# Pre-LN attention and gated MLP on one core: a head in pairs, a plan that counts copies, tails that overtake

## The chip, the cores and the metric

The kernel runs on one core of a Trainium2 chip. The metric is the device time of one execution in microseconds. Engines are named as in the profile: PE is TensorE's matrix products, PEld its weight loads, DVE is VectorE, ACT is ScalarE, POOL is GpSimd, and SP is the engine whose queue issues the transfers.

## The reference

One transformer block over 2048 rows of width 640, in bfloat16, with 32 heads of 20:

```python
h = x + mha(layernorm(x), wqkv, wo)      # softmax(q k^T / sqrt(20)) v, 32 heads
g = layernorm(h) @ w_gate                # 640 x 1728
u = layernorm(h) @ w_up                  # 640 x 1728
out = h + (g * u) @ w_down               # 1728 x 640
```

## The kernel before, in words

**Attention.** Queries are cut into four blocks of 512 rows (0 to 3), heads into eight groups of four. A segment is one group of heads for one block of queries, or for half a block (256 rows). `SPLIT_1`, `SPLIT_2` and `SPLIT_3` say how many of the eight groups of blocks 1, 2 and 3 run whole; the other groups run first for the first half of the block (segments C, E, A) and then for the second half (D, F, B). Before the change block 3 ran two groups whole and six in halves.

Scores are made in units of 128 keys by 512 queries (`emit_S`, L723), three or two units at a time. ScalarE takes the exponential of most of them (`E`, L731). Every fourth to sixth unit goes to VectorE instead, which builds the exponential from bits (L743, L626 to L631). The products with the values (`emit_AV`, L870) accumulate in one bank `acc` and are copied out when a segment closes (L900). A sum row is inverted either by a chain of transfers through memory and POOL (`norm`) or, for a few urgent segments, on TensorE (`job_norm`, L792, L807, L823).

**Order of the work.** The whole instruction order is written out by a planner in Python when the kernel is built. It keeps clocks of its own for TensorE and VectorE (`clk["pe"]`, `clk["dve"]`) and the end of each exponential (`act_end`). After each step of scores it admits other TensorE work up to `limit_of(i)`. That other work lies in a queue `jobs`: transposes of the normed rows (`job_T`), projections of q, k and v (`job_proj`, `job_dense`, `job_V`), and the tails. `HURRY` adds 100 ns to the limit in block 3. Where no job can run, `idle_products` issues products whose results are not used (L1409, and L285 with `ident`). TensorE takes its queue strictly in the order written, so a job that waits also holds the scores behind it.

**Tails.** When every group of a block or half block is normed, `add_tail` appends a tail: loads of x and of the first weights (`load_tail` L1119, `load_w` L1175), the output product with the residual (`job_out`, L1132) and the second layer norm, the gated products (`job_glu`, L1202, results L1234) and the down product (`job_y`, L285 with `hh`, added at L1272, stored at L1279). Tails run one after the other in that queue.

**Head.** The first four row tiles are normed in two pairs. Each is transposed (L322), and then the first q and k products of group 0 run for both pairs (L972). They land in `pQ` and `pK` and are copied out in one piece of 512 columns each (L261 on ScalarE, L263 on VectorE). `WARM` products on the identity (L937) come before all of this; `pad` (L212) spreads the weights.

**End.** After the last exponential a loop flushes the value products and gives leftover jobs a turn (`work`). `last_tail` then does the tail of the last 256 rows: output products (L1332, L1334, L1338), the layer norm, transposes, glu (L1202 into `f`) and y. Between the norm's statistics and its application (L242) `fill()` runs all jobs left over.

Of the kernel before, what the change touches and what calls it, by code (L numbers as in the profile page):

```python
# [10 lines left out]
BF16 = mybir.dt.bfloat16  # L11
# [27 lines left out]
FP = 7  # L39
# [10 lines left out]
SPLIT_3 = 2  # L50
# [6 lines left out]
WARM = 40  # L57
# [15 lines left out]
EASE, HURRY = 0, 100  # L73
# [13 lines left out]
def kernel(  # L87
# [122 lines left out]
    def pad(c):  # L210
        fn = nc.gpsimd.tensor_copy if c > 2 else nc.scalar.copy
        fn(wpad[c][:, :, :, 0:DH], wqk_half(c, 0)[:, :, 0:GP * HPG * DH].rearrange("p m (h e) -> p m h e", e=DH))  # L212
# [117 lines left out]
    def job_lnT(t):  # L330
        yield from job_T(lns[t], lnT[:, :, t * P:(t + 1) * P])

# [6 lines left out]
    def job_proj(m, g, ch):  # L339
        yield ROUND * KT  # L340
        ps = bank()
        for c in range(KT):
            by_cols(ps[:], wslice(m, g, c), lnT[:, c, ch * QB:(ch + 1) * QB], start=(c == 0), stop=(c == KT - 1))
            mm(ROUND)
            if c == KT - 1:
                evac_b("dve", kT[g][:, ch * QB:(ch + 1) * QB] if m else q_of(g, ch, 0, QB), ps[:], m)
                ev(QB, held["slot"])
            else:
# [4 lines left out]
    def job_dense(m, t, ch):  # L353
        yield ROUND * KT
        ps = bank()
        for c in range(KT):
# [47 lines left out]
    def job_V(t, half):  # L404
        yield 136 * KT
        ps = bank()
        for c in range(KT):
# [8 lines left out]


# [162 lines left out]
    def can_work(limit):  # L580
# [5 lines left out]
        start = max(clk["pe"], next_free()) + (SWITCH if clk["kind"] != "cols" else 0)  # L586
# [24 lines left out]
    def acc_rounds(i):  # L611
# [8 lines left out]
        return int(max(when(u) for _, u in got) <= clk["pe"] + SLACK)  # L620
# [208 lines left out]
    def when(u):  # L829
        return u[0] if u[4][0] == "d" else act_end[u[0]] + WAKE  # L830
# [15 lines left out]
    def emit_AV(i, rounds, flush=False, need=None):  # L846
        while rounds > 0 and acc["next"] < len(segs):
# [12 lines left out]
            clk["pe"] = max([clk["pe"]] + [when(u) for _, u in got])  # L860
            mm(ROUND * w // QB)
            rounds -= w / QB
            for q, u in got:
# [3 lines left out]
                ensure(("v", kt, g // (NG // 2)))  # L867
# [83 lines left out]

    for k in range(2):
# [7 lines left out]
    pad(2)  # L960
    first_T(1, "dve", lambda: bn(pair_mv[1], 1, xs[0][:, 3, :]))
    for c in (3, 4):
        pad(c)
    m32, r = rstd_act(pair_mv[1], 2)
    for k in range(2):
        apply1(2 + k, m32, r, k)
    first_T(2, "act")
    first_T(3, "dve")
    for pr in range(2):
        for m in (1, 0):  # L970
            for c in range(KT):
                nc.tensor.matmul(  # L972
                    (pQ, pK)[m][:, pr * HW:(pr + 1) * HW], lhsT=wslice(m, 0, c),
                    rhs=lnT[:, c, pr * HW:(pr + 1) * HW], start=(c == 0), stop=(c == KT - 1))
    warm = small.tile([P, 1], BF16, name="warm", tag="den")
    nc.scalar.activation(warm[:], ones[:], ACT.Exp)
    load_x(2)
    evac_b("act", kT[0][:, 0:QB], pK[:, 0:QB], 1)
    evac_b("dve", q_of(0, 0, 0, QB), pQ[:, 0:QB], 0)
# [110 lines left out]
    def open_late():  # L1090
# [8 lines left out]
        nc.vector.tensor_copy(late["if"][:], ident[:])  # L1099
# [449 lines left out]
```

## Time and profile before

| | us |
|---|---|
| median of 3 runs | 881.75 (880.72 to 882.86) |
| profiled execution, its time | 881.99 |
| its span, first to last instruction | 880.1 |
| PE busy | 827.3 (94%) |
| ACT busy | 799.7 (91%) |
| DVE busy | 702.9 (80%) |
| POOL busy | 190.4 (22%) |

Read it so: the span is the execution as the trace has it, and the 1.9 us between it and the execution's time lie outside of the instructions. Shares are means over stages that differ: a head without exponentials, a long loop in which ScalarE is nearly always busy, and an end in which TensorE works alone. In rows of the timeline the first number is the start, the second the duration, both in us; a bracket gives the idle time before the instruction and what ended it. In rows of stretches (start:end) the columns are the length and then busy time with instruction counts of PE, PEld, DVE, ACT and POOL, the granted TensorE clock, the DMA share and GB/s. In rows of groups the busy time and the mean ns of one instruction follow the bar. Rows of the chain have start, duration and what it was.

### The profile page before, as it was taken

The page shows a single profiled execution, that of the slowest core. Times are in us where ns is not written, and L with a number is a line of the kernel's source. Part 1 is how long each engine was busy: PE and PEld are TensorE (multiplying, and loading weights), DVE is VectorE, ACT ScalarE, POOL GpSimd, SP SyncE. Part 2 cuts the span into 40 slices and gives each one's busy share as a digit, 9 for nine tenths or more (in the row PEclk, how much of TensorE's full clock was granted, in tenths as well). Part 3 has the DMA queues.
Part 4 walks back from the last instruction along what each step waited for, and adds up shares of the span by engine and source line. Part 5 has one row for each costly group of instructions (what it writes and reads, how often), then busy time and mean ns, then how long its engine had stood idle before and what let it go on. Part 6 is the DMA issues. An engine that isn't in the chain of part 4 may idle for free.

```text
span 880.1 us, 34361 instructions
## 1 busy us (share of the span) xinstructions
PE 827.3 (94%) x15265; PEld 404.8 (46%) x15265; DVE 702.9 (80%) x1384; ACT 799.7 (91%) x710; POOL 190.4 (22%) x258
## 2 busy tenths in 40 slices
PE   7889999998999999999999999999999999999995
PEld 4333334332334334445444555555454556555774
DVE  6665779898778989888888889888888888988642
ACT  5889999999999999999999999999899999999530
POOL 2220001334413311222141214121301141113000
PEclk8989999999999999999999999999899999999999
DMA  6111230144212322201305131413510310031310
GB/s 184 33 58 46 67 94 13 34 108 124 63 56 64 115 75 61 52 10 39 97 25 140 26 98 30 116 38 105 126 35 15 106 39 23 18 92 49 81 45 19
DMA packets 93959, 57.62 MB, mean 65 GB/s; under 512 B 24236, under 2 KB 91692, under 8 KB 93804
## 3 DMA queue, kind: packets, MB, share of 16 engines
q1 hardware_dynamic: 93804, 55.36, 23.4%
q8 instruction: 121, 1.98, 0.9%
q14 instruction: 34, 0.28, 0.1%
HBM read 46.94 MB, written 8.16 MB: 63 GB/s over the span
## 4 chain that ended last, share of the span: by engine, by line
PE 48%; ACT 24%; DVE 21%; issue 5%; DMA 1%; SPq 0%; DVEq 0%; ACTq 0%
ACT E L731 24%; PE sc L723 12%; PE acc L870 10%; PE mi L1202 9%; PE mi L285 8%; DVE di L743 6%; PE mi L359 3%; DVE di L631 3%; DVE dm L626 2%; DVE st L218 2%; PE f L285 2%; PE f L1202 2%; DVE dt L628 2%; PE mi L723 1%; PE acc L1409 1%
## 5 line engine op out<-in xcount | busy, mean ns | idle before, releaser
L731 ACT ACTIVATE E<-sc 128x1536 bf16<-128x1536 f32 (+1 forms) x679 | 782.6, 1265 | 27.1 <-PE sc L723 13.4
L743 DVE TENSOR_SCALAR di<-mi 128x512 int16<-128x512 f32 x350 | 238.1, 685 | 65.9 <-PE mi L723 62.8
L870 PE MATMUL acc<-E,vx 128*32 128x256 bf16 (+1 forms) x2532 | 221.3, 315 | 2.7 <-DVE vx L256 2.1
L723 PE MATMUL sc<-qa,kT 21*128 21x256 bf16 (+1 forms) x1800 | 205.2, 320 | 13.9 <-ACT E L731 8.9
L723 PEld LDWEIGHTS <-kT 21*128 21x128 bf16 x3072 | 85.1, 91 | 219.1 <-issue 207.9
L768 POOL TENSOR_TENSOR rr<-rr,powers 128x8 f32<-128x8 f32 (+1 forms) x44 | 95.2, 2165 | 415.6 <-DMA rr<-sums 415.4
L870 PEld LDWEIGHTS <-vx 128*32 128x32 bf16 x3612 | 81.4, 95 | 106.3 <-issue 95.3
L631 DVE TENSOR_TENSOR di<-di,dm 128x1024 bf16<-128x1024 bf16 x175 | 122.9, 702 | 4.6
L723 PE MATMUL mi<-qa,kT 21*128 21x256 bf16 (+1 forms) x376 | 98.0, 311 | 2.5 <-DVE di L743 1.1
L626 DVE TENSOR_SCALAR dm<-di 128x1024 int16<-128x1024 int16 x175 | 78.9, 451 | 3.7
L870 PE MATMUL acc<-di,vx 128*32 128x256 bf16 (+1 forms) x540 | 77.8, 309 | 1.0 <-DVE di L631 0.9
L870 PE MATMUL acc<-dt,vx 128*32 128x256 bf16 (+1 forms) x540 | 78.1, 311 | 0.5 <-DVE dt L628 0.4
L628 DVE TENSOR_SCALAR dt<-di 128x1024 int16<-128x1024 int16 x175 | 75.9, 434 | 0.0
L723 PE MATMUL sc<-qb,kT 21*128 21x256 bf16 (+1 forms) x732 | 67.4, 290 | 2.8 <-ACT E L731 2.4
L285 PE MATMUL mi<-wd,hh 128*32 128x320 bf16 x1344 | 62.2, 300 | 1.0 <-DVE di L743 0.6
L1202 PE MATMUL mi<-ln2T,wg 128*32 128x256 bf16 (+1 forms) x1170 | 55.6, 298 | 1.9 <-DVE di L743 1.0
L1202 PE MATMUL mi<-ln2T,wu 128*32 128x256 bf16 (+1 forms) x1170 | 55.6, 303 | 0.9 <-DVE di L743 0.5
L285 PEld LDWEIGHTS <-hh 128*32 128x32 bf16 (+1 forms) x1456 | 45.6, 96 | 18.0 <-issue 8.1
L1202 PEld LDWEIGHTS <-wu 128*32 128x32 bf16 (+1 forms) x1190 | 32.9, 97 | 14.1 <-issue 10.1
L285 PE MATMUL mi<-kT,ident 128*32 128x512 bf16 x528 | 37.0, 382 | 2.2 <-DVE di L743 2.2
L1202 PEld LDWEIGHTS <-wg 128*32 128x32 bf16 (+1 forms) x1190 | 32.7, 96 | 13.5 <-issue 9.7
L723 PE MATMUL mi<-qb,kT 21*128 21x256 bf16 (+1 forms) x164 | 36.6, 291 | 1.1 <-DVE di L743 0.9
(129 smaller groups left out, 789.9 us busy)
## 6 DMA issues: line engine op xcount, KB each, us to landing
wu<-in_B_w_up_dram SPq DMA_DIRECT2D x29, 320.0 KB
wg<-in_B_w_gate_dram SPq DMA_DIRECT2D x29, 320.0 KB
dense<-dn SPq DMA_DIRECT2D x36, 128.0 KB
bc<-scr SPq DMA_DIRECT2D x64, 64.0 KB
bc<-scr SPq DMA_DIRECT2D x112, 32.0 KB
xr<-in_A_x_dram SPq DMA_DIRECT2D x16, 160.0 KB
out_dram<-xr SPq DMA_DIRECT2D x14, 160.0 KB
wd<-in_B_w_down_dram SPq DMA_DIRECT2D x13, 160.0 KB
```

Source lines behind the costliest of these rows:

```text
L218: nc.vector.bn_stats(st[:, h, :], halves[h] if halves else src[:, h * HALF:(h + 1) * HALF])
L285: nc.tensor.matmul(out[k:k + w, :], lhsT=lhsT[:, k:k + w], rhs=rhs, **flags)
L359: nc.tensor.matmul(ps[k:k + SLOT, :], lhsT=wqk_half(c, col // HALF)[:, m, col % HALF:col % HALF + SLOT], rhs=lnT[:, c, ch * QB:(ch + 1) * ...
L626: nc.vector.tensor_scalar(m16[:, 0:n], s16, M_MASK, M_BITS, ALU.bitwise_and, ALU.bitwise_or)
L628: nc.vector.tensor_scalar(t16[:, 0:n], s16, E_MASK, E_BITS, ALU.bitwise_and, ALU.bitwise_or)
L631: nc.vector.tensor_tensor(sb[:, 0:n], sb[:, 0:n], mb[:, 0:n], ALU.mult)
L723: nc.tensor.matmul(dst[:, h * w:(h + 1) * w], lhsT=kT[g][SLOT * j:SLOT * j + VS, (kt + h) * P:(kt + h + 1) * P], rhs=q_of(g, b, c0, w)[SLO ...
L731: nc.scalar.activation(e[:, 0:n], sc[:, 0:n], ACT.Exp, bias=EXP_BIAS, scale=SM_SCALE)
L743: nc.vector.tensor_scalar(t[:, k * BANK:(k + 1) * BANK], sd[:], EXP_A, 0.0, ALU.mult, ALU.max)
L768: nc.gpsimd.tensor_tensor(ri, r16, powers[:, 1:2].to_broadcast([P, n]), ALU.pow)
L870: nc.tensor.matmul(acc["t"][SLOT * j:SLOT * (j + 1), 0:w], lhsT=vx[kt][:, VS * h:VS * h + SLOT], rhs=e, start=(j not in acc["new"]), stop= ...
L1202: nc.tensor.matmul(ps[r0 + x:r0 + x + d, col:col + n], lhsT=wt[:, c, f0 + x:f0 + x + d], rhs=st["ln2T"][:, c, c0:c0 + n], start=(c == 0), ...
```

## The change

It has five parts. In the head, q and k products run by pairs of row tiles, with evictions by halves in banks of their own, three of five weight copies on POOL, the table for the exponential loaded beside the second square root, and more identity products (64 and 24 for 40). The planner counts when copies land: transposes, projections and values set `ready`, and the jobs that read them move its clock (`arrive`) or are held back (`can_work`, `acc_rounds`). A tail whose predecessor but one is finished puts its loads and its output product ahead of the queue (`urgent`); it loads its first weights early only if the glu of the tail before is done. Block 3 runs all eight groups in halves (`SPLIT_3` 0), and `HURRY` is 0. At the end VectorE's rest goes ahead of the value products, leftover jobs get a turn only after the last of them, and the leftover slots are divided: two before the norm is applied, the rest behind the last transposes. `ln2T` and `hh` are allocated once.

```diff
-SPLIT_3 = 2
+SPLIT_3 = 0
-WARM = 40
+WARM = 64
+WARM_2 = 24
-EASE, HURRY = 0, 100
+EASE, HURRY = 0, 0
...
     def pad(c):
-        fn = nc.gpsimd.tensor_copy if c > 2 else nc.scalar.copy
+        fn = nc.gpsimd.tensor_copy if c > 1 else nc.scalar.copy
...
     def job_lnT(t):
         yield from job_T(lns[t], lnT[:, :, t * P:(t + 1) * P])
+        ready["T", t] = ring["free"][held["slot"]]
+
+    def arrived(ts):
+        return max([ready.get(("T", t), 0) for t in ts])
+
+    def arrive(ts):
+        clk["pe"] = max(clk["pe"], arrived(ts))
...
     def job_dense(m, t, ch):
         yield ROUND * KT
         ps = bank()
+        arrive(chunk(ch))
...
-        start = max(clk["pe"], next_free()) + (SWITCH if clk["kind"] != "cols" else 0)
+        start = max([clk["pe"], next_free()] + [ready.get(k, 0) for k in needs.get(cur["key"], ())]) + (SWITCH if clk["kind"] != "cols" else 0)
...
-        return int(max(when(u) for _, u in got) <= clk["pe"] + SLACK)
+        for _, u in got:
+            if value_of(s, u) not in done:
+                if waiting() <= AVLOW:
+                    return 0
+                ensure(value_of(s, u))
+        return int(max(when(s, u) for _, u in got) <= clk["pe"] + SLACK)
...
+    def first_qk(pr, m):
+        for c in range(KT):
+            nc.tensor.matmul(
+                (pQ, pK)[m][:, pr * BANK:pr * BANK + HW], lhsT=wslice(m, 0, c),
+                rhs=lnT[:, c, pr * HW:(pr + 1) * HW], start=(c == 0), stop=(c == KT - 1))
+
+    def first_evac(pr, m, eng):
+        dst = kT[0][:, pr * HW:(pr + 1) * HW] if m else q_of(0, 0, pr * HW, HW)
+        evac_b(eng, dst, (pQ, pK)[m][:, pr * BANK:pr * BANK + HW], m)
...
-    for c in (0, 1):
+    for c in range(KT):
         pad(c)
     for k in range(2):
         apply1(k, m32, r, k)
     first_T(0, "act")
-    pad(2)
-    first_T(1, "dve", lambda: bn(pair_mv[1], 1, xs[0][:, 3, :]))
-    for c in (3, 4):
-        pad(c)
-    m32, r = rstd_act(pair_mv[1], 2)
+    first_T(1, "act", lambda: bn(pair_mv[1], 1, xs[0][:, 3, :]))
+    for k in range(WARM_2):
+        nc.tensor.matmul(idle[:, 0:P], lhsT=ident[:], rhs=ident[:], start=True, stop=True)
+    m32, r = rstd_act(pair_mv[1], 2, exp_table)
     for k in range(2):
         apply1(2 + k, m32, r, k)
+    first_qk(0, 1)
     first_T(2, "act")
     first_T(3, "dve")
-    for pr in range(2):
-        for m in (1, 0):
...
+    first_qk(0, 0)
+    first_qk(1, 0)
+    first_qk(1, 1)
     load_x(2)
-    evac_b("act", kT[0][:, 0:QB], pK[:, 0:QB], 1)
-    evac_b("dve", q_of(0, 0, 0, QB), pQ[:, 0:QB], 0)
+    first_evac(0, 1, "act")
+    first_evac(0, 0, "act")
+    first_evac(1, 0, "dve")
+    first_evac(1, 1, "dve")
...
-            for fp in range(2):
+            for fp in range(2 if early else 0):
                 load_w(fp, tail_st[b])
...
-        do(("load",) + key, loads)
-        add(("out",) + key, lazy(lambda st: job_out(On[b % 2], st, ts, key)))
+        out = lazy(lambda st: job_out(On[b % 2], st, ts, key))
+        last2 = seen["tails"][-2:]
+        if len(last2) == 2 and ("y",) + last2[0] in done:
+            loads(("glu",) + last2[1] in done)
+            urgent.append((("out",) + key, out, None))
+        else:
+            do(("load",) + key, loads)
+            add(("out",) + key, out)
+        seen["tails"].append(key)
...
-        fill()
+        fill(2)
...
             run(job_T(ls[t], st["ln2T"][:, :, t * P:(t + 1) * P], "act"))
+        fill()
...
+        dve_fill(act_end[i], True)
         emit_AV(i, 2, True)
-        work(i)
-        dve_fill(act_end[i], True)
+        if acc["next"] == len(segs):
+            work(i)
```

More of the change, by code (lines that the diff above doesn't have):

```diff
@@ L1099, in open_late @@
         nc.vector.tensor_copy(late["if"][:], ident[:])
+        late["ln2T"] = late["h"].tile([P, KT, QB], BF16, name="ln2T")
+        late["hh"] = [late["h"].tile([P, 2, QB], BF16, name=f"hh{f}") for f in range(FP)]
+        nc.gpsimd.memset(late["hh"][-1][M1:P, 1, :], 0.0)
         late["Wd"] = [late["wd"].tile([P, D], BF16, name=f"wd{f}") for f in range(2 * FP)]
@@ L1415, in idle_products @@
             mm(ROUND)
[L1417 removed]
+    seen = {"t": 0, "last": False, "tails": []}
     i = 0
```

43 lines of the change are left out of this document (23 added, 20 removed).

## The prediction

> **What bounds the kernel now.** I read the page first, then the busy time by stretches, then the timeline at both ends and where stretches showed a hole.
>
> ```profile
> span 880.1 us, 34361 instructions
> PE 827.3 (94%) x15265; PEld 404.8 (46%) x15265; DVE 702.9 (80%) x1384; ACT 799.7 (91%) x710; POOL 190.4 (22%) x258
> ...
> PE 48%; ACT 24%; DVE 21%; issue 5%; DMA 1%; SPq 0%; DVEq 0%; ACTq 0%
> ...
> L731 ACT ACTIVATE E<-sc 128x1536 bf16<-128x1536 f32 (+1 forms) x679 | 782.6, 1265 | 27.1 <-PE sc L723 13.4
> ```
>
> The 679 exponentials of L731 take 782.6 us of 880.1. TensorE looks as busy, but part of that is filler (below). Stretches of the attention loop, with ScalarE's time in the fourth pair:
>
> ```profile
> 10.00:13.00 3.00, 2.12 (x16) 1.82 (x17) 1.46 (x4) 1.49 (x3) 0.00 (x0) 0.50 1.04 336
> ...
> 17.67:35.00 17.33, 14.70 (x226) 5.53 (x226) 10.02 (x25) 14.24 (x13) 2.63 (x5) 1.00 0.17 48
> ...
> 57.00:68.40 11.40, 9.09 (x83) 3.08 (x86) 4.68 (x11) 7.39 (x8) 0.84 (x2) 0.70 0.01 1
> 68.40:700.00 631.60, 605.79 (x11123) 272.77 (x11115) 531.95 (x1003) 615.97 (x536) 144.41 (x138) 0.99 0.26 68
> ```
>
> From 68.4 to 700 ScalarE is idle 631.60 - 615.97 = 15.6 us over 536 exponentials, 29 ns each. There is little to win there. The losses lie elsewhere: before the first exponential, 3.1 us up to 35, 4.0 us in 57 to 68.4, and the end, where no exponential runs.
>
> **Head.** The timeline before the first exponential:
>
> ```profile
> 1.35 4.45 PE L937 MATMUL mi<-ident 128*128 128x128 bf16 x40 [1.35 <-POOL ones L190]
> ...
> 5.29 0.17 DVE L922 CAST mvb<-mv 128x4 bf16<-128x4 f32 x1
> ...
> 8.16 1.38 POOL L212 COPY wp<-wqk 128x640 bf16<-128x640 bf16 x2 [4.03 <-DMA wqk<-in_A_wqkv_dram]
> ...
> 8.94 0.62 DVE L922 CAST mvb<-mv 128x4 bf16<-128x4 f32 x1
> ...
> 9.94 0.20 ACT L928 ACTIVATE den<-ve 128x2 bf16<-128x2 bf16 x1 [0.80 <-DVE ve L926]
> ...
> 11.63 0.69 ACT L254 COPY lnT<-mi 128x640 bf16<-128x640 bf16 x1 [1.49 <-PE mi L322]
> 11.92 4.47 PE L972 MATMUL sc<-lnT,wp 128*128 128x256 bf16 x20
> ...
> 12.34 1.28 ACT L976 ACT_TABLE_LOAD   x1
> 13.64 0.20 ACT L976 ACTIVATE warm<-ones 128x1 bf16<-128x1 bf16 x1
> ...
> 16.43 0.75 DVE L263 TENSOR_SCALAR qa<-sc,qv 128x512 bf16<-128x512 f32 x1 [3.78 <-PE sc L972]
> ...
> 17.67 1.45 ACT L731 ACTIVATE E<-sc 128x1536 bf16<-128x1536 f32 x1 [1.62 <-PE sc L723]
> ```
>
> Now all twenty K and Q products of L972 follow the transposes of tiles 2 and 3 and take 4.47 us, 0.224 each, at the granted clock of 0.50. Then one 512-column eviction (0.75) and the scores stand before the exponential. The change runs the five K products of the first pair ahead of those transposes, the five Q products of that pair while ScalarE copies tile 2, and only ten after it. It evicts by halves of 256 columns, shared by ScalarE and VectorE.
>
> The tile-2 copy itself comes later than its 11.63. POOL's weight copies cost 0.69 each (1.38 for two). VectorE's cast, 0.17 at 5.29, took 0.62 at 8.94 and ended at 9.56, as POOL's second copy did (9.54). A third POOL copy holds it some 0.2 us longer. The table load moves between the square root (10.14, then some 10.3) and that copy: 1.28 + 0.20 puts the copy at 11.9 to 12.6. VectorE's removed tile-1 copy was hidden by this wait, so it saves nothing. Then five Q products at full clock, half of 0.224 each, 0.6; a half eviction, about 0.4; scores and start, 17.67 - 17.18 = 0.5. The first exponential stands at 14.1: **3.5 us gained**. At clock 0.50 it is 0.6 less for five products plus 0.2 for the scores: 2.7. Bounds: 2.0 (half clock and one more 0.69 on VectorE) and 4.1 (no hold by POOL).
>
> The 24 extra and 24 more warm-up products cost nothing where they sit in TensorE's idle time. At 0.11 each (4.45/40), the first 64 end at 8.5 at worst, before the cast of 8.94 for which the second pair waits.
>
> Two rules of the Trainium skill bear on this. The row says that the load and what followed it took 13.64 - 12.34 = 1.30. The page "ScalarE: Activation LUTs", section "What ACT_TABLE_LOAD costs", gives a switch of tables about 2.66 us, a drain included; by it the copy would wait 1.4 longer and the head would gain 2.1. This trace shows no such drain. The clock row shows 0.50 after a stretch of little but transposes. The page "TensorE: Matmul & The Clock Gate", section "Part 4: PE-mode transpose", says that transposes do not count as busy time for the clock; by that the 24 products decide, and the gain is 3.5 or 2.7.
>
> **Counting when copies land.** The hole at 57 to 68.4:
>
> ```profile
> 62.02 0.49 DVE L256 COPY lnT<-mi 128x640 bf16<-128x640 bf16 x1
> ...
> 62.56 1.47 PE L359 MATMUL mi<-lnT,wqk 128*32 128x512 bf16 x12 [0.85 <-DVE lnT L256]
> ...
> 64.68 1.02 ACT L731 ACTIVATE E<-sc 128x1024 bf16<-128x1024 f32 x1 [2.33 <-PE sc L723]
> ```
>
> TensorE waits 0.85 for a copy of lnT, then runs twelve dense products, and the scores behind them in its queue leave ScalarE idle for 2.33. With the copy's time in the plan, the scores go first. I take 2.2 of the 4.0 idle; bounds 0 (the stall moves) and 4.0. In 17.67 to 35 the same rule could win or lose some of 3.1; I take nothing, as the waits there are for results that the next step needs.
>
> **Tails, block 3 in halves, end.** F is the tail of block 2's second half, A that of block 3's first. Their last normalisations, F's first loads, and the filler from 633 to 826 as groups:
>
> ```profile
> 632.60 0.42 DVE L823 TENSOR_TENSOR on<-asb,mi 128x256 bf16<-128x256 f32 x1 [0.71 <-PE mi L807]
> ...
> 691.45 1.59 SPq L1119 DMA_DIRECT2D xr<-in_A_x_dram  x2
> ...
> 761.97 0.40 DVE L823 TENSOR_TENSOR part<-asb,mi 128x256 bf16<-128x256 f32 x1
> ...
> L1409 PE MATMUL acc<-kT,zeros 128*32 128x256 bf16 (+1 forms) x152 | 6.2, 280 | 0.0
> ...
> L285 PE MATMUL mi<-kT,ident 128*32 128x512 bf16 x68 | 4.9, 382 | 0.0
> ```
>
> F's sums were ready at 632.6 but its loads went out at 691.45, when the tail before it was through. While a tail's loads and layer norm run, TensorE has nothing and multiplies filler: 6.2 + 4.9 = 11.1 us. Overtaking puts the out products and norm of the next tail in front, so that glu and y work fills those holes. The end:
>
> ```profile
> 823.17 2.60 ACT L731 ACTIVATE E<-sc 128x1024 bf16<-128x1024 f32 x2
> ...
> 825.20 2.36 PE L1202 MATMUL mi<-ln2T,wres 128*32 128x256 bf16 x80
> ...
> 827.38 0.61 PE L870 MATMUL acc<-E,vx 128*32 128x256 bf16 x16
> 827.82 3.99 PE L1202 MATMUL mi<-ln2T,wres 128*32 128x256 bf16 x140
> ...
> 831.74 0.31 PE L1332 MATMUL f<-xr,ident 128*128 128x320 bf16 x1
> ...
> 837.58 7.77 PE L285 MATMUL f<-wd,hh 128*128 128x320 bf16 x56
> ...
> 840.84 0.16 DVE L932 RECIPROCAL rstd<-den 128x1 f32<-128x1 bf16 x1 [0.27 <-ACT den L928]
> ...
> 845.79 0.79 DVE L242 TENSOR_SCALAR ln<-xr,m,rstd 128x640 bf16<-128x640 bf16 x2
> ...
> 848.11 1.14 PE L1202 MATMUL f<-ln2T,wres 128*128 128x256 bf16 x9 [1.02 <-ACT ln2T L254]
> ```
>
> Halves make A ready at half of block 3: 632.6 plus half of the 193 us to the last exponential's end (825.77), about 730 instead of 762. After that end 2.36 + 3.99 us of A's glu and 7.77 of its y remain, 14.1. Less 11.1 of filler, 3.0 remain, under two of the four y slots (1.94 each). Then the last value products start at 825.9, the out stage at about 826.6 instead of 831.74, and it ends 5.8 later (837.58 - 831.74) at 832.4. The norm's rstd was ready at 841.0, 3.4 after that stage, but VectorE's adds for y stood ahead of the apply until 845.79. With two slots the apply comes at 836.8 and the last glu 2.3 later, at 839.1 instead of 848.11: 9.0. I take **8.0**, since not each hole will fit a job. Bounds: 1.1, if no filler is replaced and only the two slots move behind the transposes; 10.0, if no y is left and the apply follows rstd at once. What is late next is the last glu, whose length does not change.
>
> **What it adds.** Where glu of the tail before is not done, an overtaking tail does not load its weights early. SP then issues them behind the output store of that tail's y, and TensorE's queue, with the next scores in it, waits for them. Nearest landings from the chain, and an issue:
>
> ```profile
> 0.73 2.37 DMA xs<-in_A_x_dram
> ...
> 55.29 3.59 DMA kT<-dense
> ...
> 693.14 0.38 SPq L1175 DMA_DIRECT2D wu<-in_B_w_up_dram  x1
> ```
>
> A VectorE add (taken as the 0.49 copy at 62.02), an issue (0.38) and 2.37 are 3.2; one exponential queued on ScalarE (1.27) covers some, so 2.0 are left. F pays it, A perhaps, as F's glu may be done by then: 3.0. The load from HBM is nearest to the first row. Bounds: 0, and twice (0.49 + 0.38 + 3.59 - 1.27), 6.4. Halves add two normalisations, with some 14 more DMA issues on SP and two inversions on POOL, which is busy 22%, and two copies of acc that block its next segment: 0.4, from 0 to 2.0. The sharing of ln2T and hh, one memset instead of four, and the 100 ns of HURRY come at nothing: they touch POOL or shift a limit by a constant.
>
> **Sum.** -3.5 - 2.2 - 8.0 + 3.0 + 0.4 = -10.3. The profiled execution took 881.99 (span 880.1), 0.24 above the median of 881.75; so 871.7 against it, 871.5 against the median.
>
> **Rivals.**
> Tails are held by the slots between scores, not by missing work: holes stay, and only the flush order (1.5 at 825.9 against 827.38) and the 1.1 come. For it: TensorE is busy 605.79 of 631.60, and fill is let in only up to a limit that ScalarE's end sets. Against: 11.1 us of filler. The same holds if the overtaking condition is not met. -3.5 - 2.2 - 2.6 + 3.0 + 0.4 gives 876.8. Chance 0.22.
> The clock halves again in the head (0.8) and in the last norm, where a gap of 3.3 without products comes before the last glu, whose first 5 us would take twice 2.5: 874.8. Chance 0.10. The clock page of the Trainium skill, section "What's actually happening", puts the half clock after an idle window of about 3.4 us; this trace shows it at the head, and none at the end, where products are dense.
> The table load holds ScalarE 1.4 longer: 872.9. Chance 0.02. This is the rule of the page "ScalarE: Activation LUTs" in the Trainium skill.
> Slower: the new plan puts scores later throughout, as its clock now jumps to landings that really come sooner, and value products wait for jobs they draw in. ScalarE's gap of 29 ns doubles: 679 x 30 ns = 20.4, time 891.9. It decides from 15 ns each (10.3/679). For: every fill step is placed anew. Against: lower HURRY gives scores more room in block 3. Chance 0.09.
> All at the good ends: -4.1 - 4.0 - 10.0, 863.7. Chance 0.07.
> The forecast keeps 0.50.
>
> The range 865 to 878 holds forecast, held tails, clock and table, and leaves out the good ends and the slower case, 0.16. A change under 0.2%, 1.8 us, cannot be told from none here: 0.03, from the edge of the held tails and a half-size drift. Faster 0.88, slower 0.09.
>
> **What would show it.** Right: first exponential near 14, clock 1.00 from 10 to 14; no 2-us wait of ScalarE near 62; filler from 633 to 826 under half of 11.1; no L1202 products between the last two groups of value products; the apply of the last norm after two y slots, under 12 us behind the last exponential. Wrong: glu products still after the last exponential, waits of TensorE for wu at F or A over 3 us, or more than 29 ns between exponentials.

## The result, and the profile after

The changed kernel is slower: 886.65 us (median) against 881.41 for the kernel before in the same runs, ratio 1.0063 (95% interval 1.0043 to 1.0084). The forecast was 871.5, with 0.88 on faster. Medians are over all executions, ratios here and below leave out the few slow ones, over 1.5% above the fastest of their kernel (two of ten in y2, two of 29 of the kernel before, none here). The profiled execution took 883.22, 3.4 below the median of its kernel, so that the profile shows less loss than the median does. The page of the changed kernel:

```profile
span 881.4 us, 34684 instructions
...
L750 ACT ACTIVATE E<-sc 128x1536 bf16<-128x1536 f32 (+1 forms) x679 | 783.0, 1261 | 33.8 <-PE mi L742 15.3
```

Here and below, E0, E75 and so on are the exponentials of ScalarE by their index. Six stretches of the kernel before, cut at the starts of E0, E75, E150, E400 and the last one, E678:

```profile
0.00:17.67 17.67, 11.20 (x87) 8.98 (x91) 10.44 (x38) 8.39 (x14) 4.89 (x59) 0.81 0.73 219
17.67:111.70 94.03, 88.05 (x1239) 32.56 (x1235) 60.96 (x130) 86.67 (x76) 9.58 (x18) 0.96 0.17 50
111.70:198.20 86.50, 83.78 (x1227) 29.79 (x1223) 74.55 (x137) 85.47 (x77) 20.24 (x11) 1.00 0.24 63
198.20:493.60 295.40, 280.52 (x4882) 119.27 (x4878) 250.99 (x471) 287.54 (x252) 79.75 (x77) 1.00 0.26 69
493.60:824.30 330.70, 318.83 (x7282) 178.27 (x7274) 285.81 (x563) 321.45 (x279) 75.69 (x93) 0.99 0.25 66
824.30:880.10 55.80, 44.86 (x579) 35.94 (x576) 20.14 (x50) 10.19 (x18) 0.22 (x1) 0.97 0.09 26
```

The same stretches of the changed kernel:

```profile
0.00:15.43 15.43, 12.08 (x135) 10.83 (x139) 10.33 (x38) 8.37 (x15) 5.72 (x60) 1.00 0.81 237
15.43:105.50 90.07, 86.32 (x1218) 33.16 (x1214) 59.66 (x128) 85.54 (x75) 9.60 (x18) 0.98 0.16 48
105.50:194.20 88.70, 84.99 (x1234) 30.80 (x1230) 74.52 (x138) 86.53 (x76) 17.93 (x11) 1.00 0.25 69
194.20:491.50 297.30, 282.69 (x4880) 119.15 (x4876) 251.39 (x472) 288.26 (x252) 79.02 (x76) 0.99 0.26 69
491.50:829.30 337.80, 318.22 (x7612) 183.90 (x7604) 291.29 (x573) 321.20 (x279) 80.18 (x97) 0.98 0.25 66
829.30:881.40 52.10, 39.92 (x365) 30.38 (x355) 14.54 (x41) 10.23 (x19) 0.22 (x1) 0.93 0.10 28
```

Read the first number behind each stretch. The head is 2.2 shorter and the way to E75 4.0 shorter. Up to E400, 2.2 and 1.9 of these 6.2 are given back. From E400 to the last exponential 7.1 are lost, and the end wins 3.7. ScalarE is busy for the same 321 us in the fifth stretch of both kernels, so the 7.1 are idle time of ScalarE.

**Where the 7.1 lie.** Between E400 and E450 (491.5 to 558.9) the changed kernel needs 67.4 us, the one before 58.5 (493.6 to 552.1). Its timeline there, and TensorE around it as stretches:

```profile
521.91 5.99 ACT L750 ACTIVATE E<-sc 128x1536 bf16<-128x1536 f32 x5
...
524.35 0.36 SPq L1311 DMA_DIRECT2D out_dram<-xr  x1
524.75 1.12 SPq L1207 DMA_DIRECT2D wu<-in_B_w_up_dram  x1
...
528.86 0.84 PE L1234 MATMUL mi<-ln2T,wu 128*32 128x256 bf16 x24 [2.46 <-DMA wu<-in_B_w_up_dram]
...
530.72 1.02 ACT L750 ACTIVATE E<-sc 128x1024 bf16<-128x1024 f32 x1 [2.82 <-PE sc L742]
```

```profile
526.19:529.60 3.41, 0.95 (x31) 0.73 (x32) 1.09 (x3) 1.71 (x2) 0.17 (x1) 1.00 0.87 231
529.60:536.40 6.80, 6.80 (x104) 3.03 (x96) 2.91 (x6) 3.71 (x4) 0.00 (x0) 0.50 0.51 133
```

This is D, the tail of block 1's second half. It overtakes C while C's glu is unfinished, so its first weights are not loaded early. SP issues them right behind the output store of C's y. The glu products stand in TensorE's queue and wait 2.46 for wu, the scores stand behind them, and ScalarE is idle for 2.82. Then the granted clock falls to 0.50 for 6.8 us. F waits too, 1.1 us at 695. A, which the forecast named as the second one that might pay, has its weights in time.

**The head:**

```profile
9.68 1.28 ACT L987 ACT_TABLE_LOAD   x1
9.69 0.73 PE L977 MATMUL sc<-lnT,wp 128*128 128x256 bf16 x5
...
11.05 2.02 PE L977 MATMUL sc<-lnT,wp 128*128 128x256 bf16 x15
...
13.10 0.47 ACT L262 ACTIVATE kT<-sc,kb 128x256 bf16<-128x256 f32 x1 [1.34 <-PE sc L977]
...
13.97 0.48 DVE L264 TENSOR_SCALAR qa<-sc,qv 128x256 bf16<-128x256 f32 x1 [2.23 <-ACT qa L262]
...
15.43 2.37 ACT L750 ACTIVATE E<-sc 128x1536 bf16<-128x1536 f32 x2 [1.49 <-PE sc L742]
```

The products run at full clock, 2.02 for fifteen, as forecast. But the eviction of the first pair's K, complete near 10.4, starts only when all twenty products have ended (13.07), and VectorE's first one waits for ScalarE's second. The first exponential comes at 15.4, not 14.1.

**The end**, with the filler from 633 to 826 as groups:

```profile
L1452 PE MATMUL acc<-kT,zeros 128*32 128x256 bf16 x144 | 5.6, 275 | 0.0
...
L286 PE MATMUL mi<-kT,ident 128*32 128x512 bf16 x32 | 2.1, 382 | 0.0
```

```profile
830.84 0.40 PE L893 MATMUL acc<-E,vx 128*32 128x256 bf16 x7 [0.99 <-ACT E L750]
...
831.10 1.60 PE L286 MATMUL mi<-wd,hh 128*32 128x320 bf16 x37
...
842.59 0.80 DVE L243 TENSOR_SCALAR ln<-xr,m,rstd 128x640 bf16<-128x640 bf16 x2
...
843.80 5.57 PE L286 MATMUL f<-wd,hh 128*128 128x320 bf16 x28
...
849.21 1.04 PE L1234 MATMUL f<-ln2T,wres 128*128 128x256 bf16 x8
```

The order is as intended: no glu of a tail between the last two groups of value products, and the norm is applied 11.8 behind the last exponential (842.59 - 830.78). But of 11.1 us of filler 7.7 remain. So a good part of A's y is left over: 86 of its products run behind the last exponential, where the kernel before had 56 of y and 196 of glu. The last 28 of them stand ahead of the last glu and take 5.57 us, the first 3.3 of them at clock 0.50. The last glu starts 18.4 behind the last exponential (849.21 - 830.78); the forecast had 13.3, the kernel before 22.3.

### The profile page after: what moved, and what is told of

It is laid out like the page before. It is cut to its first block, busy times and chain, and to the rows that moved or that the text cites. A ratio compares the mean times of both kernels' runs of the same rounds, so it can differ in the third digit from the quotient of the medians.

```text
span 881.4 us, 34684 instructions
## 1 busy us (share of the span) xinstructions
PE 824.2 (94%) x15411; PEld 408.2 (46%) x15411; DVE 701.7 (80%) x1386; ACT 800.1 (91%) x711; POOL 192.7 (22%) x262
## 5 line engine op out<-in xcount | busy, mean ns | idle before, releaser
L742 PE MATMUL sc<-qa,kT 21*128 21x256 bf16 (+1 forms) x1800 | 207.1, 323 | 16.2 <-ACT E L750 10.4
L787 POOL TENSOR_TENSOR rr<-rr,powers 128x8 f32<-128x8 f32 (+1 forms) x46 | 97.3, 2115 | 424.7 <-DMA rr<-sums 424.7
L893 PEld LDWEIGHTS <-vx 128*32 128x32 bf16 x3764 | 87.5, 96 | 107.5 <-issue 95.4
L893 PE MATMUL acc<-dt,vx 128*32 128x256 bf16 (+1 forms) x564 | 76.1, 306 | 0.1
L742 PE MATMUL sc<-qb,kT 21*128 21x256 bf16 x836 | 67.9, 273 | 2.4 <-ACT E L750 1.9
L286 PE MATMUL mi<-wd,hh 128*32 128x320 bf16 (+1 forms) x1388 | 66.3, 301 | 0.5 <-DVE di L762 0.3
L1234 PE MATMUL mi<-ln2T,wg 128*32 128x256 bf16 (+1 forms) x1210 | 57.4, 302 | 1.5 <-DVE di L762 1.0
L286 PEld LDWEIGHTS <-hh 128*32 128x32 bf16 (+1 forms) x1486 | 47.5, 97 | 17.5 <-issue 7.4
L1234 PEld LDWEIGHTS <-wu 128*32 128x32 bf16 (+1 forms) x1230 | 33.1, 96 | 18.1 <-issue 10.0
L742 PE MATMUL mi<-qb,kT 21*128 21x256 bf16 x188 | 36.0, 271 | 1.4 <-DVE ln2T L257 0.7
L257 DVE CAST u<-mi 128x512 bf16<-128x512 f32 x49 | 33.5, 684 | 3.1 <-PE mi L1234 2.8
```

Of the source, the lines that this page charges most:

```text
L257: nc.vector.tensor_copy(dst, src)
L286: nc.tensor.matmul(out[k:k + w, :], lhsT=lhsT[:, k:k + w], rhs=rhs, **flags)
L742: nc.tensor.matmul(dst[:, h * w:(h + 1) * w], lhsT=kT[g][SLOT * j:SLOT * j + VS, (kt + h) * P:(kt + h + 1) * P], rhs=q_of(g, b, c0, w)[SLO ...
L787: nc.gpsimd.tensor_tensor(ri, r16, powers[:, 1:2].to_broadcast([P, n]), ALU.pow)
L893: nc.tensor.matmul(acc["t"][SLOT * j:SLOT * (j + 1), 0:w], lhsT=vx[kt][:, VS * h:VS * h + SLOT], rhs=e, start=(j not in acc["new"]), stop= ...
L1234: nc.tensor.matmul(ps[r0 + x:r0 + x + d, col:col + n], lhsT=wt[:, c, f0 + x:f0 + x + d], rhs=st["ln2T"][:, c, c0:c0 + n], start=(c == 0), ...
```

## The experiments

The ratio is to the kernel before, run beside it on the same chip. E75, E400 and E678 are starts in the profiled execution. "Ahead" means late weights loaded ahead. The kernel before ran again with each group of runs, at medians between 879.75 and 881.41, so the ratios are compared and not the medians.

| kernel | us | ratio (95%) | E0 | E75 | E400 | E678 | span |
|---|---|---|---|---|---|---|---|
| before (profile above) | 881.41 | 1 | 17.7 | 111.7 | 493.6 | 824.3 | 880.1 |
| changed | 886.65 | 1.0063 (1.0043-1.0084) | 15.4 | 105.5 | 491.5 | 829.3 | 881.4 |
| x1 ahead | 876.92 | 0.9970 (0.9939-1.0000) | 15.7 | 105.7 | 492.2 | 824.3 | 875.0 |
| x2 no overtaking | 889.95 | 1.0124 (1.0076-1.0171) | 16.2 | 106.0 | 491.4 | 820.9 | 886.1 |
| x4 no halves | 891.41 | 1.0131 (1.0089-1.0173) | 15.7 | 106.0 | 492.3 | 837.0 | 889.5 |
| x5 head of before | 885.97 | 1.0075 (1.0044-1.0105) | 16.5 | 105.0 | 490.0 | 833.5 | 883.8 |
| y1 overtaking alone | 898.32 | 1.0211 (1.0158-1.0263) | 16.9 | 107.7 | 494.2 | 839.5 | 894.3 |
| y5 overtaking, ahead | 885.04 | 1.0047 (1.0027-1.0068) | 16.1 | 111.6 | 496.7 | 834.2 | 889.5 |
| y3 filler in the wait | 883.99 | 1.0048 (1.0007-1.0089) | 16.1 | 107.7 | 493.0 | 828.8 | 879.2 |
| y4 ahead, no halves | 883.39 | 1.0043 (1.0011-1.0075) | 16.2 | 107.8 | 493.6 | 828.0 | 880.2 |
| y2 no counting | 885.55 | 1.0042 (1.0009-1.0076) | 16.0 | 109.4 | 491.1 | 833.8 | 884.6 |
| z1 ahead, no counting | 880.27 | 1.0006 (0.9974-1.0039) | 15.8 | 107.7 | 489.3 | 823.1 | 875.2 |
| z2 ahead, prompt evictions | 877.95 | 0.9978 (0.9954-1.0002) | 14.4 | 104.7 | 488.9 | 821.5 | 871.8 |
| z3 as z2, no counting | 877.40 | 0.9950 (0.9924-0.9977) | 14.6 | 106.8 | 491.9 | 825.7 | 878.0 |
| c2 ahead, head of before | 877.04 | 0.9967 (0.9941-0.9993) | 16.5 | 105.2 | 490.6 | 822.5 | 874.7 |
| c3 ahead, no head, no counting | 876.61 | 0.9965 (0.9934-0.9995) | 16.8 | 111.8 | 494.8 | 827.8 | 878.6 |

### The late weights: x1, y1, y5, y3

**x1** loads an overtaking tail's first weights as soon as the glu before it has released their buffers, ahead of that tail's y. Only the order on SP differs.

```diff
-            loads(("glu",) + last2[1] in done)
+            ahead = ("glu",) + last2[1] in done
+            loads(ahead)
+            if not ahead:
+                k = next(n for n, j in enumerate(jobs) if j[0] == ("y",) + last2[1])
+                needs[("w01",) + key] = {("glu",) + last2[1]}
+                jobs.insert(k, (("w01",) + key, once(lambda: [load_w(fp, tail_st[b]) for fp in range(2)]), None))
```

> The changed kernel, with the first weights of an overtaking tail loaded as soon as the glu of the tail before it is done (ahead of that tail's y) and not behind its output store. Every engine but SP keeps its order. Theory 1 (late weights: TensorE's queue waits 2.45 us for wu at D and 1.1 at F, the wait at D is followed by 6.8 us at half clock, and ScalarE runs dry): no wait for wu in the trace, the exponential of index 450 comes 5 to 7 us earlier against that of index 400, and the time falls by 5 to 9 us against the changed kernel, ratio to the kernel before about 0.999. Rival 2 (the clock: fewer filler products leave TensorE under the clock's threshold at many places, and the wait is only one of them): the two waits go, 2 to 3 us, and the ratio stays at 1.003 or above.

The timeline of x1 at the same place, and its stretch from E400 to E678:

```profile
498.46 0.40 SPq L1207 DMA_DIRECT2D wu<-in_B_w_up_dram  x1
...
526.37 0.84 PE L1234 MATMUL mi<-ln2T,wu 128*32 128x256 bf16 x24 [0.28 <-DVE ln2T L257]
...
527.86 7.21 ACT L750 ACTIVATE E<-sc 128x1024 bf16<-128x1024 f32 x6 [0.26 <-PE sc L742]
```

```profile
492.20:824.30 332.10, 315.90 (x7612) 184.03 (x7604) 290.43 (x573) 321.44 (x280) 79.14 (x97) 0.99 0.26 67
```

The wait of 2.46 and the half clock are gone, the stretch takes 332.1 instead of 337.8, and the time falls by 0.93% (1.0063 / 0.9970), 8.2 us. The late weights turned a small gain (0.3%, its interval reaching 1.0000) into the loss.

**y1** puts the overtaking alone into the kernel before, with the sharing of `ln2T` and `hh` that it needs, and **y5** adds x1's edit to y1.

```diff
...
+        last2 = seen["tails"][-2:]
+        if len(last2) == 2 and ("y",) + last2[0] in done:
+            loads(("glu",) + last2[1] in done)
+            urgent.append((("out",) + key, out, None))
...
```

> The kernel before with one part of the change alone: a tail's output products are put in at once when the tail before last has given its y, and the glu weights wait until the last tail's glu is done. Head, plan, halves and end are those of before. Theory 1 (the late weights are the loss): block 1's second tail, whose turn comes while the tail before it still computes glu, waits over 2 us for wu in TensorE between 520 and 535; ScalarE stands idle over 2 us there; a stretch of half clock follows; exponentials 400 to 450 take 65 to 68 us instead of 58.5; the time is 4 to 9 us above before, 885 to 891. Rival (overtaking pays for itself at the end of the last block, and the loss in the full change comes from another of its parts): 400 to 450 within 2 us of 58.5 and the time within 2 us of before, or below it.

> The kernel before with the overtaking of a tail's output products, and with the two weight loads that come late put ahead of the last tail's y transfers; head, plan, halves and end of before. It differs from the run of overtaking alone (898.3, 1.0211) by the order of loads on SP only. Theory 1 (nearly all that overtaking alone costs is the late weights, 4.36 us of waiting in TensorE at 533 and 3.67 at 708, with the half clock behind each): no wait for wu over 1 us, exponentials 400 to 450 in 60 to 63 us, 550 to 575 under 31, time 883 to 888, still 0.3 to 0.9% above before since the rest of the overtaking brings nothing without halves. Rival (overtaking is a loss by itself, through what it does to the order of the tails): 890 or more with no wait for wu.

The waits of y1:

```profile
PE mi L1200 <- DMA wu<-in_B_w_up_dram: 8.0, 2, 4.4
```

D and F wait for 8.0 us together, and y1 is 2.1% slower, 898 where I had given at most 891. With the weights ahead no such wait is left, and y5 is 1.6% faster than y1 (1.0047 / 1.0211), inside what was expected. The remaining 0.5% are the overtaking's own: without halves it wins nothing.

**y3** keeps the weights late, but lets TensorE compute while it waits: 64 products that nothing reads, ahead of the glu of D (44) and F (20; `by_cols` writes four products each time).

```diff
+        for _ in range(st.pop("fill", 0)):
+            by_cols(ps[:], ident[:], kT[0][:, 0:QB], start=True, stop=True)
...
+        if order[0] == 0 and ("w", 0) not in st:
+            st["fill"] = 11 if st is tail_st[1] else 5
```

> The changed kernel with 64 added 128x512 products that nothing reads, put into the glu bank ahead of the glu products of the two tails whose weights come late (44 at block 1's second tail, 20 at block 2's), so that TensorE computes through the wait for wu instead of standing still. By some 0.22 us each they take the 2.5 and 1.1 us that it waits, and more. Theory 1a (the wait itself is the smaller part, the half clock behind it the larger): no half clock between 525 and 545, exponentials 400 to 450 take 60 to 64 us instead of 67.4, time 3 to 5 us below the changed kernel. Theory 1b (the wait costs what it costs, through the queue of scores that runs dry, and the half clock adds little): 400 to 450 within 2 us of 67.4, or longer for the added products, time within 2 us of the changed kernel or above it. Rival (the half clock near 530 is not set by the wait): it stays though TensorE computes throughout.

One row of its timeline and its stretches from E400 to E450 and around D:

```profile
532.37 7.22 ACT L750 ACTIVATE E<-sc 128x1024 bf16<-128x1024 f32 x6 [2.89 <-PE sc L742]
```

```profile
493.00:557.90 64.90, 60.97 (x1452) 35.52 (x1444) 54.18 (x106) 58.08 (x51) 15.95 (x18) 0.97 0.30 80
526.30:540.90 14.60, 13.05 (x285) 7.73 (x283) 9.38 (x19) 10.28 (x10) 1.35 (x2) 1.00 0.59 157
```

Here the clock stays at 1.00 around D. Over all traces it is the same: in the five kernels whose weights come late and that have no such filler (changed, x4, x5, y1, y2) a stretch of half clock begins between 525 and 531; in the kernel before, the other nine runs and y3 none begins between 510 and 600. So the half clock follows from the wait. ScalarE is still idle for 2.89.

From E400 to E450 the kernels need 67.4 (changed), 64.9 (y3) and 61.4 (x1). Not all of the 6.0 between the first and the last belongs to the wait. The same stretch cut at E425, of the changed kernel and then of x1:

```profile
491.50:523.20 31.70, 29.68 (x689) 16.20 (x680) 27.27 (x57) 29.31 (x26) 8.74 (x12) 0.95 0.08 23
523.20:558.90 35.70, 31.49 (x727) 18.63 (x723) 27.15 (x50) 28.90 (x27) 7.22 (x7) 0.90 0.48 126
492.20:522.90 30.70, 28.44 (x690) 16.25 (x682) 26.98 (x57) 29.18 (x26) 9.07 (x12) 1.00 0.25 66
522.90:553.60 30.70, 28.80 (x724) 17.96 (x720) 27.00 (x50) 28.82 (x26) 7.48 (x7) 1.00 0.39 102
```

The wait lies behind 526. So 1.0 of the 6.0 comes before it, with a half clock at 502.3 that this execution of x1 does not have; y3 and c2 have it and need 31.8 there. What lateness costs at D is the rest, 5.0. In y3 the second part takes 33.1, and 30.2 to 30.7 in the eight kernels that overtake without the wait. So some 2.5 of the 5.0 go with the half clock, and some 2.5 stay although TensorE is busy. The added products have a part in these (44 of them are some 2.9 us of work, estimated from the 2.1 that 32 such products took above), so this split is rough. The stretch, 64.9, lies between what 1a (60 to 64) and 1b (65.4 or more) expected. The time, 0.15% or 1.3 us below the changed kernel, is within the 2 us of 1b, but with intervals of 0.2 and 0.4% on each side it decides nothing.

### Overtaking and halves: x2, x4, y4

```diff
 x2: the changed kernel without overtaking
-        if len(last2) == 2 and ("y",) + last2[0] in done:
+        if False:
 x4: the changed kernel with block 3 as before; y4: the same on x1
-SPLIT_3 = 0
+SPLIT_3 = 2
-EASE, HURRY = 0, 0
+EASE, HURRY = 0, 100
```

> The changed kernel without overtaking: each tail queues its loads and its output products behind the tail before, as in the kernel before. Theory 1: no wait for wu at D or F, filler from 500 to 830 comes back to over 8 us, leftover work at the end grows by 6 to 8 us, ratio about 1.000 to 1.004 (head and plan keep 6 us, the stalls go, the end pays). Rival 2: with filler back the clock stays up, and the ratio is 0.990 to 0.995.

> The changed kernel with block 3 as before: two groups whole, six in halves, and HURRY 100. Theory 1: the stall at D stays, the end is 3 to 5 us later since A is ready later, ratio 1.009 to 1.012. Rival 3 (halves cost more than they bring: more acc copies and norms): ratio under 1.004.

> The changed kernel with its late weights loaded ahead of the y transfers, as in the run that took 876.9, and with the last block in two whole groups instead of halves, with the hurry of before. Theory 1 (halves are worth what they were costed at, the spared leftovers of the end less 0.4): without halves the stretch after the last exponential is 53 to 57 us against 50.7 with halves, and the time 2 to 5 us above 876.9, so 879 to 882. Rival (the halves' added weight loads and evictions eat up what the end gains): the time within 1.5 us of 876.9 or below it.

The ends of x2 and of y4, from the last exponential on, and the waits of x4:

```profile
820.90:886.10 65.20, 52.01 (x838) 42.15 (x826) 23.70 (x55) 10.21 (x19) 0.22 (x1) 0.97 0.19 53
```

```profile
828.00:880.20 52.20, 40.98 (x431) 31.84 (x419) 18.31 (x48) 10.14 (x19) 0.22 (x1) 0.96 0.10 28
```

```profile
PE mi L1234 <- DMA wu<-in_B_w_up_dram: 6.5, 2, 4.2
```

Without overtaking (x2) the exponentials end earliest of all, at 820.9, but 838 products are left for the end, which takes 65.2 us. That is 13 more than in the changed kernel and not the 6 to 8 expected, and the time missed what both theories of x2 expected (at most 1.004). Without halves F waits 4.2 us for its weights instead of 1.1 (x4), so x4, at 1.0131 a little above what theory 1 expected, mixes two causes. y4 is free of the wait: halves (with `HURRY` 0) are worth 0.73% (1.0043 / 0.9970), 6.4 us, more than the 2 to 5 expected. The two parts need each other: both with weights ahead 0.9950 to 1.0006 (six kernels), overtaking with weights ahead but without halves 1.0043 and 1.0047, halves without overtaking 1.0124, neither 1. No run prices the new order of the end by itself. But y4 has it, with the changed head and the counting, and y5 has none of the three, and the two differ by 0.04%.

### Head and counting: x5, y2, z1, z2, z3, c2, c3

x5, c2 and c3 have the lines of the head as before. y2, z1, z3 and c3 take the counting out (two of its places shown):

```diff
-        clk["pe"] = max(clk["pe"], arrived(ts))
+        pass
...
-        start = max([clk["pe"], next_free()] + [ready.get(k, 0) for k in needs.get(cur["key"], ())]) + (SWITCH if clk["kind"] != "cols" else 0)
+        start = max(clk["pe"], next_free()) + (SWITCH if clk["kind"] != "cols" else 0)
...
```

> The changed kernel with the head of the kernel before; the rest of the program keeps its order. If the head's gain lasts to the end, the time is 3 to 6 us above the changed kernel, ratio 1.010 to 1.013, and the exponential of index 75 comes 3 to 6 us later. Rival 4 (the gain is swallowed by later waits for transfers and for the clock): first exponentials 2 to 4 us later, but the exponential of index 200 at the same time as in the changed kernel, ratio 1.006.

> The changed kernel with the plan's counting of copies taken out again: no wait for an arrival in the plan, value products are not put behind their value chunk, the rest as changed. The changed kernel has its 75th exponential at 105.5 against 111.7 before, and its 200th at 254.4 against 257.1, so that 3.5 of 6.2 us are gone by then. Theory 1 (the counting gave the lead of the first stage, and the time lost from 75 to 200 is lost for another reason, a pause of TensorE near 212 and the half clock behind it): exponential 75 at 110 to 112, 75 to 200 between 145 and 149, time 1 to 6 us above the changed kernel, 888 to 893. Rival (the counting only moves work: what it wins up to 75 it gives back up to 200, because the filler and the value products that it puts elsewhere come due later): exponential 75 at 110 to 112, 200 at 254 to 255, and the time within 2 us of the changed kernel.

> The changed kernel with its late weights ahead (876.9, 0.997) and with the plan's counting of copies taken out. Theory 1 (the counting only moves work within the first 400 exponentials and is worth nothing at the end): exponential 75 near 109 instead of 105.7, 400 within 1 us of 492, time within 2 us of the kernel with the weights ahead and the counting. Rival (the counting is worth its lead): 879 to 881.

**z2** keeps each pair's K and Q in one tile and evicts the first pair ahead of the second pair's products:

```diff
...
     first_qk(0, 0)
+    first_evac(0, 1, "act")
+    first_evac(0, 0, "dve")
     first_qk(1, 0)
     first_qk(1, 1)
     load_x(2)
-    first_evac(0, 1, "act")
-    first_evac(0, 0, "act")
     first_evac(1, 0, "dve")
-    first_evac(1, 1, "dve")
+    first_evac(1, 1, "act")
...
```

> The changed kernel with its late weights ahead, and in the head with a pair's K and Q products in one tile of their own and that pair's two evictions behind them, ahead of the second pair's products, one on ScalarE and one on VectorE; the order of everything else stays. In the changed kernel all four evictions wait until the last of the 20 products has ended at 13.07 and the scores begin at 15.00. Theory 1 (that queue is what the head's gain went into): the first pair's evictions at 11.8 to 12.0, the scores at 13.6 to 13.9, the first exponential at 14.0 to 14.3 instead of 15.4 to 15.7; of these 1.3 us 0 to 1.3 are kept at exponential 100, and the time is 0 to 1.3 us below 876.9. Rival (the lead is swallowed on the way, by the wait for kT near 54 and the work that the plan has placed by due times): first exponential as early, but exponential 100 and the time within 0.5 us of the kernel without this edit.

> The kernel of z2 (weights ahead, first evictions behind their own products; 877.95, 0.9978) without the plan's counting of copies. Theory 1 (the counting is worth under 1 us at the end): within 0.2% of z2's ratio, so 0.996 to 1.000. Rival (the 3 us between z1 and x1 are the counting's): 1.000 to 1.003.

> The changed kernel with its weights ahead and the head of before; counting, tails, halves and end as changed. Theory 1 (the head by pairs is worth 1 us of the 3.5 it was costed at, since the wait for kT near 54 and the plan swallow the rest): 0 to 0.2% above the kernel with the weights ahead (0.997), so 0.997 to 1.000. Rival (without the late weights in its way the head shows its whole 2.2 us of earlier first exponential and more): 1.000 to 1.002.

> The changed kernel with its weights ahead and both the head and the plan of before: of the change only the overtaking tails, the halves and the order of the end are left. Theory 1 (head and counting together are worth 0 to 2 us, the tails, halves and end the rest of what is won): 0.997 to 1.000. Rival (each is worth what x5 and z1 suggest, 1 and 3 us, and they add): 1.001 to 1.003. If it is below 0.997, one of the two makes the kernel slower.

The evictions of z2, and the head of before in c2: its twenty products, which took 4.47 in the profile of before, and its stretch, to be compared with the first one shown of before:

```profile
12.16 0.47 ACT L262 ACTIVATE kT<-sc,kb 128x256 bf16<-128x256 f32 x1
12.67 0.48 DVE L264 TENSOR_SCALAR qa<-sc,qv 128x256 bf16<-128x256 f32 x1 [0.56 <-ACT kT L262]
...
14.45 2.37 ACT L750 ACTIVATE E<-sc 128x1536 bf16<-128x1536 f32 x2
```

```profile
11.96 3.24 PE L1009 MATMUL sc<-lnT,wp 128*128 128x256 bf16 x20
...
0.00:16.50 16.50, 10.43 (x87) 8.86 (x91) 10.51 (x38) 8.38 (x15) 4.90 (x59) 1.00 0.80 232
```

**Head.** z2's evictions start 0.9 earlier than in the changed kernel, and its first exponential 1.3 before x1's; at E100 1.0 of that is left (133.0 against 134.1). The time does not show it: 0.9978 against 0.9970. The queue of evictions was part of the reason, as theory 1 said, but removing it gains nothing that can be measured. The rows of c2 tell more. There the same twenty products took 3.24 and the first exponential came at 16.5; in the profile of before they took 4.47, at half clock throughout, and it came at 17.67. (The 1.00 in c2's stretch is no measure of the old head: the first clock record of that trace is at 13.78, and the column counts what no record covers as 1.00.) The table has five executions with the old head besides that of before, c2's among them, with 3.24 to 3.83 for the twenty products and first exponentials at 16.1 to 16.9. It has eight with the changed head, at 15.4 to 16.2. So more than half of the 2.2 us is how one execution of before fell out; some 0.7 is the head's, by the means of the others (16.6 and 15.9). x5 missed both of its expectations: its E75 is 0.5 earlier than in the changed kernel and not later, and its time is 0.12% longer.

**Counting.** It does win time early: from E0 to E75 the kernels that count need 88.5 to 91.6 us, the others 90.8 to 95.5. From E75 to E150 it is the other way round: 88.7 (changed, x1, c2) against 86.4 to 87.3 (c3, before, z1). By E400 no lead is left that has one sign: 492.2 (x1, counting) against 489.3 (z1), but 488.9 (z2, counting) against 491.9 (z3). Of what was expected of y2 the rival's came nearer: its time is 1.9 us below the changed kernel's by the ratios, though its E75 (109.4) is earlier than either expected. z1 fell where its rival had it (880.27, for 879 to 881), which by itself would give the counting 3 us. z3 takes the same step from z2 and goes the other way, below what both of its theories expected (0.996).

Taking the head away changes the ratio by +0.0012 (x5 less changed), -0.0003 (c2 less x1) and -0.0041 (c3 less z1). Taking the counting away changes it by -0.0021 (y2), +0.0036 (z1 less x1), -0.0028 (z3 less z2) and -0.0002 (c3 less c2). The signs are mixed, and the interval of such a difference reaches some 0.004 to each side. Each is worth nothing within 0.3% or so, and which sign it has stays open. c3, with neither, is as fast as x1; z3 has the lowest ratio of all, 0.9950, but the median of c3, run in the same group, is lower (876.61 for 877.40).

## Why the prediction was wrong

The measured ledger, in the forecast's terms: late weights +8.2 (x1 against the changed kernel, some 3 to either side), tails, halves and end -3.1 (c3, 0.35%, some 2.7 to either side), head and counting about 0. The sum, +5.1, is near the measured +5.5 (0.63%) for the most part by construction, since x1 and c3 differ by 0.05% only. In the profiled executions the first term is smaller: the spans of the changed kernel and of x1 differ by 6.4.

- **Late weights: +3.0 forecast, +8.2 measured.** The mechanism was named and put in the right order on SP. Two things failed. It was put at F and perhaps A, but F and D pay. D's turn comes in block 1, with C's glu unfinished, and I had looked only at block 3 and its neighbour. And each wait was costed at its own 2.0 us. The wait at D was 2.46, close to that; but the queue of scores runs dry and the clock halves for 6.8 us behind it, 5.0 in all at D alone. F adds some 1.4 (E550 to E575 takes 31.3, in x1 29.9). The upper bound, 6.4 for both tails, took a longer landing but no effect on the clock.
- **Tails, halves and end: -7.6 forecast (-8.0, and +0.4 for the halves), -3.1 measured.** The forecast let 11.1 us of y and glu fill the holes; 3.4 us of filler went. The apply came as forecast, 11.8 behind the last exponential for 11.0. But the two slots in front of the norm were all that was foreseen; the slots behind the transposes, 5.57 us, stand ahead of the last glu and put it 5.1 later than forecast. Some 1.6 of these are the half clock there, which the forecast had as a rival: in x1 and c3, without it, the last glu starts at 16.8 and not 18.4. And a loss ahead of the end was not in the sum: from E400 to E678 c3 needs 333.0 and the kernel before 330.7, which takes 2.3 from the 5.0 that its end wins (50.8 for 55.8). Overtaking moves work to where ScalarE then waits: E400 to E450 takes 61.4 in x1 without any wait for weights, 58.5 before and 58.3 in x2 without overtaking, and only 0.9 of that comes back up to E650. The rival of held tails, -2.6, came near in size; its mechanism, holes that all stay, is not what the filler shows.
- **Head: -3.5 forecast, nothing measured.** Three steps failed. The eviction, put right behind the first pair's products, waits for all twenty. The price of the old head was read from one execution at clock 0.50, where the twenty products took 4.47; five others took 3.24 to 3.83. And a us gained at the first exponential was put down as a us at the end: z2 mends the eviction and starts at 14.45, near the 14.1 of the forecast, and is no faster than x1. The table load cost the copy of tile 2 at most 0.24: it takes 1.28 here too, the transposes of tile 2 end at 10.85, and the copy starts at 11.09, ahead of the forecast's 11.9 to 12.6. No drain is seen, so the page "ScalarE: Activation LUTs" of the Trainium skill, with 2.66 in its section "What ACT_TABLE_LOAD costs", is not borne out.
- **Counting: -2.2 forecast, about 0.** The stall near 62 went, as the forecast said, but another came at 55:

```profile
53.56 0.38 PE L742 MATMUL sc<-qa,kT 21*128 21x512 bf16 x1 [1.03 <-DMA kT<-dense]
...
55.25 2.36 ACT L750 ACTIVATE E<-sc 128x1536 bf16<-128x1536 f32 x2 [2.27 <-PE sc L742]
```

From E0 to E75 counting wins 1.9 to 3.3 us in three pairs of kernels (x1 and z1, z2 and z3, changed and y2) and 6.3 in a fourth (c2 and c3), which is the 2.2 of the forecast or more. It was lost from E75 on, so the step that failed is again that an early lead was taken as time at the end. In that stretch products of value chunks that the plan now draws in stand ahead of scores; that these are the cause was not tried.
- **The slower rival** (more than 29 ns between exponentials throughout) is not what happened: E150 to E400 takes 297.3 against 295.4. The largest loss is one place, D, and not a drift. The list of what would prove me wrong named waits at F and A only; the wait was at D.

## What to carry to other kernels

A step that jumps a queue must bring its loads with it: follow each load it needs to the point where it is issued, for every instance of the step, not for the one next to the stage you want to improve. Cost a wait of the engine that feeds the bottleneck at more than its length, since the queue behind it runs dry and the clock may halve; here 2.5 us cost 5. Work moved into a stretch in which the bottleneck has no slack is not free because filler disappears elsewhere, and a lead early in the run is worth only what is left of it at the last exponential.

## What the runs showed of the hardware that I had not expected

The granted clock halved after stretches in which TensorE was not idle but only partly busy, for 3.4, 6.8 or 10.2 us. Before the half clock at 529.6 it was busy for 0.95 of 3.41 us; two others in the changed kernel, ahead of 212.2 and 55.2:

```profile
208.79:212.20 3.41, 2.30 (x22) 0.62 (x21) 3.38 (x8) 2.87 (x3) 2.65 (x4) 1.00 0.77 153
51.79:55.20 3.41, 1.88 (x25) 0.55 (x17) 0.01 (x1) 1.19 (x2) 1.25 (x3) 1.00 0.24 75
```

67% and 55% busy were not enough to keep the clock here. But the share of busy time does not decide alone: the changed kernel was busy for 2.25 of the 3.41 us from 864.13, 66%, and kept the clock, and before was busy for 3.00 of 3.41 from 627.73, 88%, and lost it. What counts these runs do not show. The page "TensorE: Matmul & The Clock Gate" of the Trainium skill, section "What's actually happening", speaks of an idle window of about 3.4 us; the length agrees, the idleness does not. That the window runs free of the program, as the same section says, would fit that the twenty products of the old head took 4.47 us in before and 3.24 to 3.83 in five other executions. The times follow the clock: the executions of x1 lie between 874.0 us at 0.992 and 882.2 at 0.982, which is as much as the late weights cost.

Two evictions from different banks of one tile, by ScalarE and VectorE, ran one behind the other (12.67 behind 12.16 in z2, 13.97 behind 13.47 in the changed kernel). Whether the program or the chip orders them these runs do not show.
